# Probability-weighted sums of v with the probabilities as weights, turned back by VectorE, and the last chunk's wide visits at other places

## The chip, the cores and the metric

The kernel runs on one core of one Trainium2 chip. The metric is the time of one execution in device microseconds. TensorE (PE) multiplies, VectorE (DVE) and ScalarE (ACT) do the elementwise work, SyncE (SP) issues nearly all transfers, GpSimd (POOL) makes a few masks.

## The reference, cut to what matters

Attention over 8 batches, 8 heads, 576 positions and a head size of 64, with a window of 32 (heads 0 to 3 plain, heads 4 to 7 with a stride of 4 over 128 positions), and then a feed-forward layer on the result.

```
scores = scale * q @ k^T              # masked: 0 <= rel < 32, or 0 <= rel < 128 and rel % 4 == 0
attn   = exp(scores - max) / (sum + 1e-9)
x      = attn @ v                     # (8, 8, 576, 64), then (4608, 512)
h      = x @ w_in                     # 512 -> 2048
out    = gelu(h) @ w_out              # 2048 -> 512
```

Inputs and results are fp32. q and k are drawn so that the scores spread widely.

## The kernel before

The 4608 rows are worked on in nine chunks (c = 0 to 8) of 512 rows. Chunks 0 to 7 are the first 512 positions of a batch, chunk 8 holds the 64 positions that each batch has left. A chunk's attention is done in four pairs of heads (p = 0, 1 plain, p = 2, 3 strided), each pair in windows of 32 queries by 64 keys; in chunk 8 pairs 2 and 3 are "wide", 32 queries by 96 keys.

The feed-forward layer of a chunk is written out in four quarters of eight steps, 32 in all: eight blocks of `h` (`ffn_h_part`, L530, each block 12 matmuls of 128x512 and then a Gelu on ScalarE and a rounding split on ScalarE and VectorE), eight blocks of `o` (`ffn_o`, L557, 12 such matmuls each), eight more of `h`, and then `o` again, this time one output bank after the other, 24 matmuls each. Every product is done as three matmuls on rounded halves. `h` goes to PSUM banks 4 and 5 in turn, `o` is summed up in banks 0 to 3.

While the layer of chunk c runs, the attention of chunk c + 1 is put between its matmuls, by a list of steps that is sorted by place and then by rank (L667 to L707): `scores` at places 2 and 4 (two pairs at a time), `softmax` on ScalarE from 8.5, the norm and `turn` on VectorE from 10.5, the product with v (`av`, L475) at 24.75 for pairs 0 and 1 and at 26.75 for pairs 2 and 3, and right behind it `xout` (L500), which copies the product as a rounded half (ScalarE) and takes the rest off it (VectorE). These halves are what the next chunk's `h` reads. All queues run in the order in which this list writes them. A visit of two pairs to TensorE is called a burst here. The trace shows each fp32 matmul of the attention as two weight loads and two matmuls, so that a burst of 64 matmuls has 128 of each.

In `scores` a pair's weights are 32 queries of one head (64 rows by 32 columns) and the moving data are 64 keys. In `av` before, the weights are v of one head and window half (64 rows by 64 columns) and the moving data are 32 queries' probabilities; the result stands as head dimension by query, as the layer needs it. In chunk 8 the wide pairs' `av` takes 32 rows by 64 columns as weights, 48 matmuls for half a pair, in four visits, at 26.75 and 28.25 (pair 2) and 28.5 and 30 (pair 3). `av` writes banks 4 to 7; pair p has 128 columns of each.

Chunk 0's attention and the weights' unpacking come first, in an order written out by hand; chunks 0 and 1 use other functions (`av_wide`, `av_early`) for the product with v. The work tiles of a pair (`sm`, `turned`) rotate through seven buffers.

Of the kernel before, what the change touches and what calls it, by code (L numbers as in the profile page):

```python
# [7 lines left out]
F32 = mybir.dt.float32  # L8
# [8 lines left out]
B, H, S, D = 8, 8, 576, 64  # L17
WIN, DIL = 32, 4
DM, DFF = H * D, 2048
P = 128  # L20
# [7 lines left out]
KB, NU = 32, 4  # L28
# [50 lines left out]
def attn_ffn(ctx: ExitStack, tc: tile.TileContext, qk, qk_lp, qk_ld, v, v_ld, w, outT):  # L79
    nc = tc.nc  # L80
# [3 lines left out]
    work = ctx.enter_context(tc.tile_pool(name="work", bufs=2))  # L84
# [3 lines left out]
    ps = psum.tile([P, 8, 512], F32, name="ps")  # L88
# [7 lines left out]
    def copy(e, out, in_):  # L96
        if e == "a":
            nc.scalar.copy(out, in_)  # L98
        else:
            nc.vector.tensor_copy(out, in_)  # L100
# [133 lines left out]
    def load(s):  # L234
        yield "q"
        if s.rest:
            t = wpool.tile([P, N + NU * 4 * KL if s.wide else N + B * KL], F32, tag="w", name="raw_qk")
            src = (qk_ld if s.wide else qk_lp)[s.p % 2]
            s.raw = t
        else:  # L240
            if s.p % 2 == 0:
                held["qk", s.c, s.p // 2] = wpool.tile([P, 2, 2 * N], F32, tag="w", name="raw_qk")
            s.raw = held["qk", s.c, s.p // 2][:, s.p % 2]
            src = qk[s.c, s.p]
        nc.sync.dma_start(s.raw, src)  # L245

    def load_v(s):

        yield "q"
        t = wpool.tile([P, 2, NU, 2, 2 * D], F32, tag="w", name="v_sb")  # L250
        nc.sync.dma_start(t, v[s.c, s.p // 2])
        for i in range(2):
            o = xs[s.c][s.p + i]
            o.v = t[:, i] if s.c > 1 else t[:, i].rearrange("p u j d -> p (u j) d").rearrange("p (a r) d -> p a r d", a=2)
# [13 lines left out]
    def slot(s, u):  # L268
        return u if s.plain or s.rest or s.c < 2 else (u - 1) % NU
# [96 lines left out]
    def sum_up(s):  # L366
        yield "d"
        nc.vector.tensor_reduce(s.st[:, 1], s.all, axis=AX.X, op=ALU.add)
# [71 lines left out]
    def turn_half(s, k):  # L440

        e = yield "ad"
        rows = slice(64 * k, 64 * k + 64)
        copy(e, s.t[rows, :, k], ps[rows, s.bank].rearrange("p (i n) -> p i n", n=KB))
# [27 lines left out]
                            to = to[:, (2 * r + a) * KB:(2 * r + a + 1) * KB]  # L472
                        nc.tensor.matmul(to, s.v[rows, a, r, h * D:(h + 1) * D], t, start=True, stop=True)  # L473

    def av(s, px, u0=0):  # L475

        yield "p"
        s.px = px
        if s.wide:
            for u in range(u0, u0 + 2):  # L480
                for m in range(3):
                    for r in range(4):
                        rows = slice(32 * r, 32 * r + 32)
                        for h in range(2):
                            nc.tensor.matmul(px(r)[h * D:(h + 1) * D, u * KB:(u + 1) * KB], s.v[rows, u, m, h * D:(h + 1) * D],  # L485
                                             s.t[h][rows, 3 * u + m], start=m == 0, stop=m == 2)
            return
        for u in range(NU):
            for j in range(2):
                for r in (j, 2 + j):  # L490
                    rows = slice(r // 2 * 64, r // 2 * 64 + 64)
                    for h in range(2):
                        nc.tensor.matmul(px(r)[h * D:(h + 1) * D, u * KB:(u + 1) * KB], s.v[rows, u, j, h * D:(h + 1) * D],  # L493
                                         s.t[rows, h * NU + slot(s, u), j], start=True, stop=True)

    def px_four(p, bank):

        return (lambda r: ps[:, bank + r, p * P:(p + 1) * P]), ps[:, bank:bank + 4, p * P:(p + 1) * P]

    def xout(s, px):  # L500
        e = yield "ad" if s.c < 2 else "a"
        s.x = xg.tile([P, 2, N], F32R, tag="xg", name="x")
        if s.wide:
            put = []
            for b in range(2):
                src = px[:, :, b * 64:(b + 1) * 64].rearrange("p r (g i) -> p r g i", g=4)
                dst = [s.x[:, t].rearrange("p (r b i g) -> p r b g i", r=4, b=2, g=4)[:, :, b] for t in range(2)]
                put.append((src, dst))
        elif s.c < 2:

            px = ps[:, s.bank + 1] if s.wide_v else ps[:, s.bank:s.bank + 2, s.p % 2 * 256:s.p % 2 * 256 + 256]
            to = [s.x[:, t] if s.wide_v else s.x[:, t].rearrange("p (k n) -> p k n", k=2) for t in range(2)]
            if s.wide_v and s.plain:
                px = px.rearrange("p (b d i) -> p b d i", d=DIL, i=8)
                to = [y.rearrange("p (d b i) -> p b d i", d=DIL, i=8) for y in to]
            put = [(px, to)]
        else:
            put = [(px, [s.x[:, t].rearrange("p (r i) -> p r i" if s.plain or s.rest else "p (i r) -> p r i", r=4)
                         for t in range(2)])]
        for y, (h, l) in put:  # L520
            copy(e, h, y)
        yield "d"
        for y, (h, l) in put:
            nc.vector.tensor_sub(l, y, h)  # L524
# [59 lines left out]
    jobs = {}  # L584
# [3 lines left out]
    def one(e, fns):  # L588

        yield e  # L590
        for g in fns:
            at_once(g)

    for f in range(NF):
# [4 lines left out]
        for i, cols in enumerate(parts(f)):  # L599
            k = f"{f}.{i}" if f < HALVED else f"{f}"  # L600
# [7 lines left out]
    for c in range(3):  # L608
        for p in range(NPAIR):
            s, k = xs[c][p], f"{c}.{p}"  # L610
            jobs["qk" + k] = load(s)
            if c == 2:
                continue
            if p % 2 == 0:
                jobs["v" + k] = load_v(s)
            if c == 0:
                jobs["scores" + k] = scores(s, (4, 0, 2, 6)[p])
                jobs["av" + k] = av_wide(s)
                for i in range(2):
                    jobs[f"half{k}.{i}"] = turn_half(s, i)  # L620
            elif p % 2 == 0:
                jobs["scores" + k] = one("p", [scores(xs[c][p + i], 6) for i in range(2)])
                jobs["av" + k] = one("p", [av_early(xs[c][p + i]) for i in range(2)])
            if c == 0 or p % 2 == 0:
                jobs["low" + k] = lowest_two(s, xs[c][p + 1]) if c else lowest(s)
                jobs["sums" + k] = inverse(s)
            jobs["exp" + k] = softmax(s)
            if s.subtract:
                jobs["sub" + k] = subtract(s)
                jobs["sum" + k] = sum_up(s)  # L630
            jobs["norm" + k] = norm(s)
            jobs["turn" + k] = turn_pe(s)
            jobs["x" + k] = xout(s, None)
    for d in range(NC):
        jobs[f"store0.{d}"] = store(0, d)

# [1 line left out]
    for i in range(BURN):  # L638
        rows = slice(32 * (i % 4), 32 * (i % 4) + 32)
        nc.tensor.matmul(ps[rows, 7, 0:2 * KB], ones[rows, 0:KB], ones[rows], start=True, stop=True)  # L640
    begun, ended, wants = set(), set(), {}
    for token in SCHEDULE.split():
        name, _, times = token.partition("*")
        name, _, e = name.partition(":")
        times = int(times or 1)
        if name == "fill":
            bank = 7
            if "scores0.3" in begun:
                bank = next(k for p, k in ((0, 5), (3, 7), (2, 3), (1, 1)) if f"exp0.{p}" in ended and f"av0.{p}" not in begun)
# [20 lines left out]
    def add(c, at, rank, gen):  # L670
        steps.append((2 * NF * c + at, rank, len(steps), gen))
# [5 lines left out]
                at_once(f)  # L677
        return gen()

    A_SC, A_E, A_N, A_X, A_QK, A_V = (2, 4), 8.5, 10.5, (24.75, 26.75), 26.5, 3  # L680
    for n in range(2, NCH):
        c = n - 1
        s = xs[n]
        late = n == LAST
        for p in range(NPAIR):
            wide = late and p >= 2
            bank = 4 + 2 * (p - 2) if wide else p // 2 * 2
            if c > 1:
                add(c, (3.25 + .25 * (p % 2)) if wide else A_QK - 32 + .25 * p, 0, load(s[p]))
            add(c, A_SC[p // 2] if not wide else 8.25, 1, scores(s[p], bank))  # L690
            add(c, A_SC[p // 2] + .5 + p % 2 if not wide else 8.5 + (p - 2), 2, lowest(s[p]))
            add(c, A_E + p + (.5 if wide else 0), 3, softmax(s[p]))
            add(c, A_N + p * 1.5 + (.5 if wide else 0), 4, inverse(s[p]))
            add(c, A_N + p * 1.5 + (.5 if wide else 0), 4, norm(s[p]))
            add(c, A_N + p * 1.5 + (.5 if wide else 0), 5, turn(s[p]))
            px = px_four(p, 4)
            at = A_X[p // 2] + (1.75 * (p - 2) if wide else 0)
            for u in (range(0, NU, 2) if wide else [0]):
                add(c, at + .75 * u, 6, av(s[p], px[0], u))
            add(c, at + (1.75 if wide else .25 + p % 2 / 2), 7, xout(s[p], px[1]))  # L700
        add(c, A_V, 0, load_v(s[0]))
        if late:
            add(c, 9, 0, load_v_wide(s[2]))
            add(c, 9.25, 0, load_v_wide(s[3]))
        else:
            add(c, A_V + .25, 0, load_v(s[2]))
    steps.sort(key=lambda t: t[:3])  # L707
    at = 0
# [127 lines left out]
```

## Time and profile before

| what | value |
| --- | --- |
| time, median of 3 runs | 886.9 us (885.46 to 887.28) |
| time of the profiled execution | 885.41 us |
| its span in the profile | 883.6 us |
| TensorE busy | 871.6 us, 99% of the span |
| VectorE busy | 352.1 us, 40% |
| ScalarE busy | 380.6 us, 43% |
| granted TensorE clock, mean | 0.999 |

A line of the profile's list of groups names the line of the kernel, the engine, the operation, the tiles (out<-in), partitions by elements, the count, then busy time, mean time of one in ns, and the engine's idle time ahead of them with what ended it. PEld is TensorE's weight load, which runs beside its matmuls. A line of the timeline has the start, the length, the engine, the same names, and in brackets the idle time ahead of it.

### The profile page before, as it was taken

How to read it: one execution, taken by the hardware profiler on the slowest of the kernel's cores; microseconds unless marked ns; L12 is line 12 of the kernel's file. 1: busy time of each engine (PE TensorE's matmuls, PEld its weight loads, DVE VectorE, ACT ScalarE, POOL GpSimd, SP SyncE). 2: the span in 40 equal slices, each digit the busy share in tenths (PEclk: the TensorE clock that was granted, in tenths of full speed). 3: DMA queues.
4: the chain of work that ended last, by engine and by line, in shares of the span. 5: the costliest groups of instructions: out<-in, count | busy, mean ns of one | idle time of the engine just before them, and what ended most of it. 6: DMA issues, size and time to landing. Idle time of an engine off the chain costs nothing.

```text
span 883.6 us, 18852 instructions
## 1 busy us (share of the span) xinstructions
PE 871.6 (99%) x8304; PEld 719.4 (81%) x8304; DVE 352.1 (40%) x597; ACT 380.6 (43%) x1016; POOL 9.5 (1%) x46
## 2 busy tenths in 40 slices
PE   7999999999999999999999999999999999999998
PEld 5888888888888888888888888888888888878886
DVE  8899934621462126321552146213622163212020
ACT  7798535442363227232544235423733272314040
POOL 1000020000000000000000000000000000000000
PEclk9999999999999999999999999999999999999999
DMA  9997431003300330024000510033002410010001
GB/s 363 416 420 281 143 101 46 1 1 134 107 0 1 121 120 1 1 92 148 3 1 1 172 69 0 1 133 108 1 1 85 167 73 1 13 38 1 0 1 48
DMA packets 16930, 75.39 MB, mean 85 GB/s; under 512 B 1872, under 2 KB 2128, under 8 KB 12496
## 3 DMA queue, kind: packets, MB, share of 16 engines
q1 hardware_dynamic: 16704, 74.06, 22.5%
q8 instruction: 65, 1.06, 0.5%
q14 instruction: 17, 0.14, 0.1%
q10 hardware_dynamic: 144, 0.13, 0.0%
HBM read 64.75 MB, written 9.44 MB: 84 GB/s over the span
## 4 chain that ended last, share of the span: by engine, by line
PE 97%; DMA 2%; SPq 0%; issue 0%; DVE 0%; ACT 0%; ACTq 0%; DVEq 0%
PE ps L560 45%; PE ps L537 45%; PE ps L493 3%; PE ps L296 3%; DMA raw_w<-w 2%; PE ps L485 1%; PE ps L473 0%; PE ps L431 0%; PE ps L454 0%; SPq L245 0%; PE ps L282 0%; ACT zeroed L98 0%; SPq L166 0%; DVE spare L190 0%; DVE sm L405 0%
## 5 line engine op out<-in xcount | busy, mean ns | idle before, releaser
L560 PE MATMUL ps<-g,weight 128*128 128x512 f32 x1728 | 401.7, 390 | 0.0
L537 PE MATMUL ps<-x,weight 128*128 128x512 f32 x1728 | 401.3, 390 | 0.0
L537 PEld LDWEIGHTS ps<-x,weight 128*128 128x128 f32 x1728 | 322.9, 188 | 67.9
L560 PEld LDWEIGHTS ps<-g,weight 128*128 128x128 f32 x1728 | 322.9, 188 | 67.2
L549 DVE TENSOR_TENSOR g<-gf,g 128x512 fp32r<-128x512 f32 x144 | 99.7, 693 | 382.6 <-ACT g L98 382.5
L544 ACT ACTIVATE gf<-ps 128x512 f32<-128x512 f32 x144 | 86.1, 598 | 311.1 <-PE ps L537 311.1
L98 ACT CAST g<-gf 128x512 fp32r<-128x512 f32 x143 | 88.8, 621 | 4.5
L380 ACT ACTIVATE sm<-sm,st 128x64 f32<-128x64 f32 (+1 forms) x224 | 74.9, 337 | 0.1
L98 ACT COPY o_sb<-ps 128x512 f32<-128x512 f32 (+1 forms) x34 | 19.7, 582 | 108.4 <-PE ps L560 103.8
L524 DVE TENSOR_TENSOR x<-ps,x 128x512 fp32r<-128x512 f32 (+1 forms) x38 | 30.2, 805 | 86.8 <-ACT x L98 86.8
L98 ACT CAST x<-ps 128x512 fp32r<-128x512 f32 (+1 forms) x37 | 27.0, 749 | 58.9 <-PE ps L493 40.6
L423 DVE STREAM_TRANSPOSE turned<-sm 32x256 f32<-32x256 f32 x104 | 45.4, 436 | 2.0
L380 ACT ACTIVATION_READ_ACCUMULATOR sm<-sm,st 128x1 f32 x224 | 42.1, 188 | 0.0
L296 PEld LDWEIGHTS ps<-raw_qk 64*32 64x32 f32 x2304 | 26.0, 110 | 9.3 <-issue 5.4
L296 PE MATMUL ps<-raw_qk 64*32 64x64 f32 (+1 forms) x2304 | 30.2, 236 | 2.5 <-DMA raw_qk<-qk 2.4
L493 PEld LDWEIGHTS ps<-turned,v_sb 64*64 64x64 f32 x1664 | 25.4, 135 | 4.6 <-issue 4.6
L493 PE MATMUL ps<-turned,v_sb 64*64 64x32 f32 x1664 | 26.9, 220 | 0.0
L405 DVE TENSOR_TENSOR sm<-sm,st 128x512 f32<-128x512 f32 x30 | 20.6, 690 | 0.9
L209 DVE SCALAR_TENSOR_TENSOR weight<-raw_w,spare 128x1024 fp32r<-128x1024 uint32 (+1 forms) x17 | 19.8, 1162 | 0.4
L197 DVE SCALAR_TENSOR_TENSOR raw_w<-raw_w,spare 128x1024 uint32<-128x1024 uint32 (+1 forms) x17 | 19.6, 1155 | 0.0
L418 DVE STREAM_TRANSPOSE turned<-sm 128x512 f32<-128x512 f32 x26 | 18.5, 711 | 0.9
L338 DVE TENSOR_REDUCE st<-sm 128x8 f32<-128x512 f32 x26 | 17.8, 686 | 0.9
(77 smaller groups left out, 252.0 us busy)
## 6 DMA issues: line engine op xcount, KB each, us to landing
v_sb<-v SPq DMA_DIRECT2D x17, 1024.0 KB, 5.2
raw_qk<-qk SPq DMA_DIRECT2D x32, 512.0 KB, 6.8
raw_w<-w SPq DMA_DIRECT2D x15, 1024.0 KB, 17.6
outT<-o_sb SPq DMA_DIRECT2D x35, 256.0 KB, 2.1
mid_w<-w SPq DMA_DIRECT2D x8, 1023.5 KB, 17.6
raw_qk<-qk_ld SPq DMA_DIRECT2D x2, 1024.0 KB, 6.6
v_wide<-v_ld SPq DMA_DIRECT2D x2, 768.0 KB, 6.1
raw_qk<-qk_lp SPq DMA_DIRECT2D x2, 640.0 KB, 5.3
```

Source lines behind the costliest of these rows:

```text
L98: nc.scalar.copy(out, in_)
L209: nc.vector.scalar_tensor_tensor(weight(f)[:, 1, cols], low, 2.0 ** (-36 if f in TWICE or f in MIDDLE else -43), t.bitcast(F32), op0=ALU.m ...
L296: nc.tensor.matmul(s.sc[32 * r:32 * r + 32, h, c0:c0 + s.nk], x[:, q0:q0 + 32], x[:, k0:k0 + s.nk], start=s.c > 1, stop=s.c > 1 or u == NU ...
L380: nc.scalar.activation(t, s.sc[:, i // NU, at:at + 2 * KB] if s.c < 2 else t, AF.Exp, bias=s.st[:, 0, i:i + 1], scale=SCALE if s.c < 2 els ...
L405: nc.vector.tensor_mul(s.all, s.all, t.unsqueeze(2).broadcast_to((P, 2 * NU, 2 * KB)))
L423: nc.vector.transpose(s.t[32 * to:32 * to + 32, :, r % 2], s.all[32 * r:32 * r + 32, :, j * KB:(j + 1) * KB])
L493: nc.tensor.matmul(px(r)[h * D:(h + 1) * D, u * KB:(u + 1) * KB], s.v[rows, u, j, h * D:(h + 1) * D], s.t[rows, h * NU + slot(s, u), j], s ...
L524: nc.vector.tensor_sub(l, y, h)
L537: nc.tensor.matmul(bank, weights[f][:, t, cc * P:(cc + 1) * P], x[:, xx], start=n == 1 and i == 0, stop=n == parts and i == 2)
L544: nc.scalar.activation(gf, bank, AF.Gelu)
L549: nc.vector.tensor_sub(g[:, 1], gf, g[:, 0])
L560: nc.tensor.matmul(ps[:, d], weights[f][:, t, DM + d * P:DM + (d + 1) * P], gs[f][:, u], start=f == 0 and n == 0, stop=f == NF - 1 and n == 2)
```

## The change

In chunks 2 to 7, and in chunk 8 for the plain pairs, `av` exchanges its operands: the probabilities (64 rows by 32 columns) are the weights and v (64 rows by 64 columns) is the moving data. There are as many matmuls as before, 32 for a pair. The result stands as query by head dimension, so a new function `turn_back` transposes it on VectorE in squares of 32 by 32, from PSUM into a new work tile `y` of the seven rotating buffers: six instructions for a pair, two over all 128 partitions and four over 32, each with 256 elements in a partition. `xout` then copies and subtracts from `y` and not from PSUM. A pair's product now takes two banks (4 and 5 for pairs 0 and 2, 6 and 7 for pairs 1 and 3), 256 columns of each. The places of the plain visits stay; `turn_back` has rank 7 and `xout` rank 8, so both pairs' turns stand ahead of both pairs' subtractions. In chunk 8 the four wide visits move to 26.25, 27.5, 29 and 30.25.

```
-                for r in (j, 2 + j):
-                    rows = slice(r // 2 * 64, r // 2 * 64 + 64)
+                for k in range(2):
+                    rows = slice(64 * k, 64 * k + 64)
                     for h in range(2):
-                        nc.tensor.matmul(px(r)[h * D:(h + 1) * D, u * KB:(u + 1) * KB], s.v[rows, u, j, h * D:(h + 1) * D],
-                                         s.t[rows, h * NU + slot(s, u), j], start=True, stop=True)
+                        g = 2 * h + j
+                        nc.tensor.matmul(s.px[32 * g:32 * g + 32, k, u * D:(u + 1) * D], s.t[rows, h * NU + slot(s, u), j],
+                                         s.v[rows, u, j, h * D:(h + 1) * D], start=True, stop=True)
...
+    def turn_back(s):
+        s.y = work.tile([P, 4, NU, KB], F32, tag="sm", name="y", bufs=7)
+        def part(src, dst, d, j):
+            x = s.px[src].rearrange("p r (u d k) -> p r u d k", d=2, k=KB)[:, :, :, d]
+            y = s.y[dst].rearrange("p (r j) u q -> p r u j q", j=2)[:, :, :, j]
+            nc.vector.transpose(y, x)
+        for d in range(2):
+            yield "d"
+            part(slice(0, P), slice(0, P), d, d)
+        for g in range(4):
+            yield "d"
+            part(slice(32 * g, 32 * g + 32), slice(32 * (g ^ 1), 32 * (g ^ 1) + 32), 1 - g % 2, g % 2)
...
-    A_SC, A_E, A_N, A_X, A_QK, A_V = (2, 4), 8.5, 10.5, (24.75, 26.75), 26.5, 3
+    A_SC, A_E, A_N, A_QK, A_V = (2, 4), 8.5, 10.5, 26.5, 3
...
+        A_X = (24.75, 24.75, 26.25, 29) if late else (24.75, 24.75, 26.75, 26.75)
...
-            at = A_X[p // 2] + (1.75 * (p - 2) if wide else 0)
-            for u in (range(0, NU, 2) if wide else [0]):
-                add(c, at + .75 * u, 6, av(s[p], px[0], u))
-            add(c, at + (1.75 if wide else .25 + p % 2 / 2), 7, xout(s[p], px[1]))
+            at = A_X[p]
+            add(c, at, 6, av(s[p]))
+            if wide:
+                add(c, at + 1.25, 6, av(s[p], 2))
+                add(c, at + 1.5, 8, xout(s[p]))
+            else:
+                add(c, at + .25, 7, turn_back(s[p]))
+                add(c, at + .25 + p % 2 / 2, 8, xout(s[p]))
```

TensorE at the second burst of a chunk (pairs 2 and 3 of chunk 2), before, with the engines or transfers that an instruction waits for in brackets:

```order
L560 MATMUL ps<-g,weight 128x512 [waits Activation_49]
L560 MATMUL ps<-g,weight 128x512
L560 MATMUL ps<-g,weight 128x512 [waits DVE_49]
L560 MATMUL ps<-g,weight 128x512 x9
L493 MATMUL ps<-turned,v_sb 64x32 [waits DMAHW6_49,DVE_49]
L493 MATMUL ps<-turned,v_sb 64x32 x63
L560 MATMUL ps<-g,weight 128x512 x63
```

And now:

```order
L578 MATMUL ps<-g,weight 128x512 [waits Activation_49]
L578 MATMUL ps<-g,weight 128x512
L578 MATMUL ps<-g,weight 128x512 [waits DVE_49]
L578 MATMUL ps<-g,weight 128x512 x9
L497 MATMUL ps<-v_sb,turned 32x64 [waits DMAHW6_49,DVE_49]
L497 MATMUL ps<-v_sb,turned 32x64 x31
L497 MATMUL ps<-v_sb,turned 32x64 [waits DVE_49]
L497 MATMUL ps<-v_sb,turned 32x64 x31
L578 MATMUL ps<-g,weight 128x512 x63
```

The burst stands where it stood; its second half, pair 3, has a wait for VectorE of its own.

VectorE at the two bursts of the same chunk, before (L549 are the splits of the last `h` blocks and of the next chunk's first):

```order
L423 STREAM_TRANSPOSE turned<-sm 32x8x32 x3
L549 TENSOR_TENSOR g<-gf,g 128x512 [waits PE_49,Activation_49] x8
L524 TENSOR_TENSOR x<-ps,x 128x512 [waits Activation_49] x2
L524 TENSOR_TENSOR x<-ps,x 128x4x128 [waits Activation_49] x2
L549 TENSOR_TENSOR g<-gf,g 128x512 [waits DVE_49,PE_49,Activation_49] x3
```

And now, from the first burst to behind its subtractions:

```order
L567 TENSOR_TENSOR g<-gf,g 128x512 [waits PE_49,Activation_49] x8
L509 STREAM_TRANSPOSE y<-ps 128x2x128 [waits PE_49]
L509 STREAM_TRANSPOSE y<-ps 128x2x128
L509 STREAM_TRANSPOSE y<-ps 32x2x128 [waits DVE_49] x2
L509 STREAM_TRANSPOSE y<-ps 32x2x128 x2
L509 STREAM_TRANSPOSE y<-ps 128x2x128 [waits PE_49]
L509 STREAM_TRANSPOSE y<-ps 128x2x128
L509 STREAM_TRANSPOSE y<-ps 32x2x128 [waits DVE_49] x2
L509 STREAM_TRANSPOSE y<-ps 32x2x128 x2
L542 TENSOR_TENSOR x<-y,x 128x512 [waits Activation_49] x2
```

Twelve transposes have come in ahead of the two subtractions; the same stands at the second burst.

TensorE in the last quarter ahead of chunk 8, from the first wide visit on, before:

```order
L485 MATMUL ps<-turned,v_wide 64x32 [waits DMAHW2_49,DVE_49]
L485 MATMUL ps<-turned,v_wide 64x32 x47
L560 MATMUL ps<-g,weight 128x512 x18
L485 MATMUL ps<-turned,v_wide 64x32 x48
L560 MATMUL ps<-g,weight 128x512 x3
L485 MATMUL ps<-turned,v_wide 64x32 [waits DMAHW3_49]
L485 MATMUL ps<-turned,v_wide 64x32 x47
L560 MATMUL ps<-g,weight 128x512 x18
L485 MATMUL ps<-turned,v_wide 64x32 [waits DVE_49]
L485 MATMUL ps<-turned,v_wide 64x32 x47
L560 MATMUL ps<-g,weight 128x512 x24
```

And now:

```order
L486 MATMUL ps<-turned,v_wide 64x32 [waits DMAHW2_49,DVE_49]
L486 MATMUL ps<-turned,v_wide 64x32 x3
L486 MATMUL ps<-turned,v_wide 64x32 [waits DVE_49]
L486 MATMUL ps<-turned,v_wide 64x32 x43
L578 MATMUL ps<-g,weight 128x512 x15
L486 MATMUL ps<-turned,v_wide 64x32 x48
L578 MATMUL ps<-g,weight 128x512 x18
L486 MATMUL ps<-turned,v_wide 64x32 [waits DMAHW3_49,DVE_49]
L486 MATMUL ps<-turned,v_wide 64x32 x47
L578 MATMUL ps<-g,weight 128x512 x15
L486 MATMUL ps<-turned,v_wide 64x32 x48
L578 MATMUL ps<-g,weight 128x512 x21
```

The gaps of 18, 3 and 18 matmuls between the wide visits are 15, 18 and 15 now, the first wide visit comes 18 matmuls after the burst of the plain pairs (24 before), and it has a second wait for VectorE.

## Rows read from the trace of the kernel before

**Rows 1.** The page's first part: span, and busy time of each engine.

```profile
span 883.6 us, 18852 instructions
PE 871.6 (99%) x8304; PEld 719.4 (81%) x8304; DVE 352.1 (40%) x597; ACT 380.6 (43%) x1016; POOL 9.5 (1%) x46
```

**Rows 2.** The page's fourth part: the chain that ended last, shares by engine.

```profile
PE 97%; DMA 2%; SPq 0%; issue 0%; DVE 0%; ACT 0%; ACTq 0%; DVEq 0%
```

**Rows 3.** Timeline of TensorE's matmuls: start, length, line, tiles, count; two bursts, one scores visit.

```profile
192.87 2.20 PE L560 MATMUL ps<-g,weight 128*128 128x512 f32 x9
195.00 2.07 PE L493 MATMUL ps<-turned,v_sb 64*64 64x32 f32 x128
197.00 5.74 PE L560 MATMUL ps<-g,weight 128*128 128x512 f32 x24
202.67 2.07 PE L493 MATMUL ps<-turned,v_sb 64*64 64x32 f32 x128
204.67 14.58 PE L560 MATMUL ps<-g,weight 128*128 128x512 f32 x63
219.08 5.60 PE L537 MATMUL ps<-x,weight 128*128 128x512 f32 x24
224.62 1.48 PE L296 MATMUL ps<-raw_qk 64*32 64x64 f32 x128
226.03 5.73 PE L537 MATMUL ps<-x,weight 128*128 128x512 f32 x24
```

**Rows 4.** Groups of instructions: line, engine, operation, tiles, count, busy us, mean ns.

```profile
L493 PEld LDWEIGHTS ps<-turned,v_sb 64*64 64x64 f32 x1664 | 25.4, 135 | 4.6 <-issue 4.6
L493 PE MATMUL ps<-turned,v_sb 64*64 64x32 f32 x1664 | 26.9, 220 | 0.0
```

**Rows 5.** Timeline of TensorE's matmuls ahead of the last chunk.

```profile
763.93 2.07 PE L493 MATMUL ps<-turned,v_sb 64*64 64x32 f32 x128
765.93 5.74 PE L560 MATMUL ps<-g,weight 128*128 128x512 f32 x24
771.59 1.17 PE L485 MATMUL ps<-turned,v_wide 32*64 32x32 f32 x96
772.70 4.38 PE L560 MATMUL ps<-g,weight 128*128 128x512 f32 x18
777.01 1.17 PE L485 MATMUL ps<-turned,v_wide 32*64 32x32 f32 x96
778.11 0.96 PE L560 MATMUL ps<-g,weight 128*128 128x512 f32 x3
779.00 1.00 PE L485 MATMUL ps<-turned,v_wide 32*64 32x32 f32 x76
781.41 0.42 PE L485 MATMUL ps<-turned,v_wide 32*64 32x32 f32 x20 [1.40 <-issue]
781.76 4.37 PE L560 MATMUL ps<-g,weight 128*128 128x512 f32 x18
```

**Rows 6.** The page's third part: the queue that brings instructions.

```profile
q8 instruction: 65, 1.06, 0.5%
```

**Rows 7.** Timeline of ScalarE and VectorE behind the two bursts of Rows 3.

```profile
197.14 0.59 ACT L98 CAST x<-ps 128x512 fp32r<-128x512 f32 x1 [2.82 <-PE ps L493]
...
208.12 1.08 DVE L524 TENSOR_TENSOR x<-ps,x 128x512 fp32r<-128x512 f32 x1 [1.13 <-ACT x L98]
```

**Rows 8.** Timeline of VectorE: the four 32-partition transposes of one pair.

```profile
251.59 1.78 DVE L423 STREAM_TRANSPOSE turned<-sm 32x256 f32<-32x256 f32 x4
```

**Rows 9.** Groups of VectorE's instructions: a transpose, and one operation from PSUM, one from SBUF.

```profile
L423 DVE STREAM_TRANSPOSE turned<-sm 32x256 f32<-32x256 f32 x104 | 45.4, 436 | 2.0
L405 DVE TENSOR_TENSOR sm<-sm,st 128x512 f32<-128x512 f32 x30 | 20.6, 690 | 0.9
L418 DVE STREAM_TRANSPOSE turned<-sm 128x512 f32<-128x512 f32 x26 | 18.5, 711 | 0.9
L332 DVE SCALAR_TENSOR_TENSOR sm<-ps,masks 128x512 f32<-128x512 f32 x24 | 16.4, 684 | 0.0
```

More of the change, by code (lines that the diff above doesn't have):

```diff
@@ L473, in av_early, with av @@
                         nc.tensor.matmul(to, s.v[rows, a, r, h * D:(h + 1) * D], t, start=True, stop=True)
-    def av(s, px, u0=0):
+    def av(s, u0=0):
         yield "p"
-        s.px = px
         if s.wide:
+            s.px = ps[:, 4:8, s.p * P:(s.p + 1) * P]
             for u in range(u0, u0 + 2):
@@ L484, in av, with xout @@
                         for h in range(2):
-                            nc.tensor.matmul(px(r)[h * D:(h + 1) * D, u * KB:(u + 1) * KB], s.v[rows, u, m, h * D:(h + 1) * D],
+                            nc.tensor.matmul(s.px[h * D:(h + 1) * D, r, u * KB:(u + 1) * KB], s.v[rows, u, m, h * D:(h + 1) * D],
                                              s.t[h][rows, 3 * u + m], start=m == 0, stop=m == 2)
             return
+        bank = 4 + s.p % 2 * 2
+        s.px = ps[:, bank:bank + 2, s.p // 2 * NU * D:(s.p // 2 + 1) * NU * D]
         for u in range(NU):
             for j in range(2):
-                for r in (j, 2 + j):
-                    rows = slice(r // 2 * 64, r // 2 * 64 + 64)
+                for k in range(2):
+                    rows = slice(64 * k, 64 * k + 64)
                     for h in range(2):
-                        nc.tensor.matmul(px(r)[h * D:(h + 1) * D, u * KB:(u + 1) * KB], s.v[rows, u, j, h * D:(h + 1) * D],
-                                         s.t[rows, h * NU + slot(s, u), j], start=True, stop=True)
-    def px_four(p, bank):
-        return (lambda r: ps[:, bank + r, p * P:(p + 1) * P]), ps[:, bank:bank + 4, p * P:(p + 1) * P]
-    def xout(s, px):
+                        g = 2 * h + j
[13 more added lines that the diff above has]
+            part(slice(32 * g, 32 * g + 32), slice(32 * (g ^ 1), 32 * (g ^ 1) + 32), 1 - g % 2, g % 2)
+    def xout(s):
         e = yield "ad" if s.c < 2 else "a"
@@ L505, in xout @@
             for b in range(2):
-                src = px[:, :, b * 64:(b + 1) * 64].rearrange("p r (g i) -> p r g i", g=4)
+                src = s.px[:, :, b * 64:(b + 1) * 64].rearrange("p r (g i) -> p r g i", g=4)
                 dst = [s.x[:, t].rearrange("p (r b i g) -> p r b g i", r=4, b=2, g=4)[:, :, b] for t in range(2)]
@@ L517, in xout @@
         else:
-            put = [(px, [s.x[:, t].rearrange("p (r i) -> p r i" if s.plain or s.rest else "p (i r) -> p r i", r=4)
-                         for t in range(2)])]
+            put = [(s.y.rearrange("p r u q -> p r (u q)"),
+                    [s.x[:, t].rearrange("p (r i) -> p r i" if s.plain or s.rest else "p (i r) -> p r i", r=4) for t in range(2)])]
         for y, (h, l) in put:
@@ L632, in attn_ffn @@
             jobs["turn" + k] = turn_pe(s)
-            jobs["x" + k] = xout(s, None)
+            jobs["x" + k] = xout(s)
     for d in range(NC):
@@ L695, in attn_ffn @@
             add(c, A_N + p * 1.5 + (.5 if wide else 0), 5, turn(s[p]))
-            px = px_four(p, 4)
-            at = A_X[p // 2] + (1.75 * (p - 2) if wide else 0)
-            for u in (range(0, NU, 2) if wide else [0]):
-                add(c, at + .75 * u, 6, av(s[p], px[0], u))
-            add(c, at + (1.75 if wide else .25 + p % 2 / 2), 7, xout(s[p], px[1]))
+            at = A_X[p]
[6 more added lines that the diff above has]
+                add(c, at + .25 + p % 2 / 2, 8, xout(s[p]))
         add(c, A_V, 0, load_v(s[0]))
```

## The prediction

> **What bounds the kernel now.** I read the busy times first: TensorE is busy for 871.6 of 883.6 us, VectorE for 40% and ScalarE for 43% [rows 1]. The chain of work that ended last then says the same of the end: 97% of it is TensorE, and no other engine has one per cent of it [rows 2]. So an edit counts by what it takes from TensorE's queue or makes that queue wait, and work on VectorE is free as long as TensorE doesn't wait for it. Third, TensorE's timeline around one chunk, which gives each kind of visit its price, start to start of what follows: the burst of two pairs of `av` takes 195.00 to 197.00, 2.00 us, and the visit of two pairs of `scores` 224.62 to 226.03, 1.41 us, for as many weight loads and matmuls, 128 each [rows 3]. Fourth, the same timeline ahead of chunk 8, which holds a place where TensorE stood still [rows 5].
>
> **The new burst.** The list of groups has 1664 matmuls in `av` at L493, 128 to a burst, so 13 bursts: two in each of chunks 2 to 7 and one in chunk 8 [rows 4]. The change keeps their count and exchanges the operands. The new shape, weights of 64 by 32 and 64 columns of data, is just the shape of `scores` [rows 3], down to one PSUM bank for each half of the rows. What differs is the order: `scores` changes the half of the rows at each matmul, the new loop at every second. The wide visits of chunk 8 also do two matmuls in a row on the same rows, and take 771.59 to 772.70, 1.11 us, for 96 [rows 5], which is 1.48 us for 128. So the burst lies between 1.41 and 1.48 us; I take 1.41, since `scores` has the very tile. Gain: 13 x (2.00 - 1.41) = 7.7 us (6.8 us with 1.48). All of it lies on the path.
>
> **The wide visits.** The first two took 1.11 and 1.10 us. The third began at 779.00, stopped after 76 of 96, waited 1.40 us for nothing that the profile shows, and let the next work begin at 781.76: 2.76 us, 1.65 us too long [rows 5]. It is the visit that came only 3 large matmuls behind another. The queue that brings instructions moved 65 packets [rows 6], and TensorE's 8304 matmuls and 8304 loads [rows 1] are 65 times 256: I read the stop as TensorE running out of instructions, with some 350 of them used up in the 3.0 us from 777.01 to 780.0. Now 15, 18 and 15 large matmuls lie between the visits. A gap of 18 had no stop [rows 5]; one of 15 isn't in the trace and lies nearer to 18 than to 3. I take the whole stop as gone: 1.65 us gained, with nought as the other end.
>
> **VectorE's new work.** Six transposes a pair, 26 pairs. Four transposes of 256 elements take 1.78 us back to back [rows 8], 0.445 us each; one over 128 partitions of 512 elements takes 711 ns against 436 [rows 9], so 256 elements cost the same on 32 or on 128 partitions within what these rows show. That is 26 x 6 x 0.445 = 69 us on an engine that is 60% idle. The rows are all from SBUF, and the new ones read PSUM; the nearest pair of rows is an operation of 512 elements from PSUM, 684 ns, beside one from SBUF, 690 ns [rows 9], so I add nothing. [...]
>
> **The waits it adds.** The instruction order shows two for TensorE. Say a first burst starts at S. Pair 0's half ends 0.7 us later, plus 0.22 us for the last matmul [rows 4] and 0.07 us to the reader (ScalarE began at 197.14 after an end at 197.07 [rows 3, 7]): VectorE begins at S + 1.0 and, with twelve transposes, is done at S + 6.3. The second burst starts behind 24 large matmuls, 197.00 to 202.67, 5.67 us [rows 3], so at S + 7.1, and its second half, which is what waits for the twelfth transpose, at S + 7.8. Slack: 1.4 us, and no wait. Queued behind that wait would be all of TensorE's work; it starts to cost at (7.8 - 1.1) / 12 = 0.56 us a transpose. Ahead of chunk 8 it is closer: the first wide visit comes 18 large matmuls behind the burst, 772.70 to 777.01, 4.31 us [rows 5], so at S + 5.7, and its fifth matmul writes a bank that pair 1's transposes read until S + 6.3, seen by TensorE at about S + 6.4. Cost: 0.7 us, once (nothing if a transpose takes under 0.39 us).
>
> Further on nothing is late. Today's subtractions end at 208.12 + 1.08 = 209.2 and the next `h`, which needs them, starts at 219.08 [rows 3, 7]; twelve transposes, two copies and two subtractions behind the second burst take about 7.5 us from its end, with 14.4 us to that `h`. The copies hold back one store of an output bank behind them on ScalarE by 2 us, and that bank is next written at 224.62. The seven rotating buffers get 12 tiles a chunk in place of 8; the buffer that `y` takes was last read by transposes or a burst ahead of it. No transfer moves past another on SP, and POOL has nothing to do with it.
>
> **Sum.** -7.7 - 1.65 + 0.7 = -8.6 us. The profiled execution took 885.41 us with a span of 883.6; its span should come to 875.0 and its time to 876.8. It lay 1.5 us below the median of the runs, 886.9, so for the median I say **878.3 us**.
>
> **Rivals.**
> *VectorE becomes the wait (slower).* Place: the second half of the second burst in chunks 2 to 7, and the first wide visit. With t us a transpose each of the six second bursts waits 12t - 6.7, the wide visit 12t - 4.7. The gain ahead of waits is 9.3 us, so it turns to a loss from t = 0.64 on. If reading PSUM in squares paid the 275 ns twice that 256 elements cost between the two rows for transposes [rows 9], t = 0.72, the waits are 6 x 1.9 + 3.9 = 15.5 us, the sum is +6, and the time 893. For it: no row has a transpose from PSUM. Against: the operations that do read it cost no more.
> *The burst doesn't get faster.* If its pace hangs on the order of the rows and not on the tile, which `av` before and after share, only the stop goes: -1.65 + 0.3 for the wide wait, 885.6. Against: the wide visits have that order too, at 11.6 ns a matmul in place of 15.6.
> *The burst halves.* Eight tiles for four would make it 1.00 us: 13.0 + 1.65 - 0.8, 873. Against: `scores` has the eight tiles already and takes 1.41 [rows 3]. [...]
> *The stop stays.* A gap of 15 may still be too short, or the shorter bursts ahead may shift where it falls: -7.7 + 0.7, 879.9.
>
> **How the numbers follow.** Forecast, with its own bounds for burst and wait, 0.80; the stop stays 0.07; VectorE late 0.06, of which 0.04 beyond the point where it is a loss; no faster burst 0.05; the burst halves 0.02. A measurement of this kernel can tell about 0.2%, 1.8 us, from no change. So faster: 0.80 + 0.07 + 0.02 + 0.02 = 0.91; same: the unchanged burst, 0.05; slower: 0.04. The forecast's own range is 877.5 (no wide wait) to 879.9 (burst at 1.48, PSUM dearer); the median of three runs lay within 1.5 us of each. So 876.0 to 881.0, which takes in the stop that stays.
>
> **What would show it.** In the new profile: bursts of L497 that take 1.41 to 1.48 us; VectorE's twelve transposes done 6.3 us after a burst's start, at about 0.445 us each, and no wait of TensorE for them at the second bursts; one wait of some 0.7 us in the first wide visit; four wide visits of 1.1 us and no idle time without a releaser; VectorE busy for about 420 us. Wrong is the prediction if the burst stays near 2 us, if L497 waits for VectorE in each chunk, or if a stop turns up in a burst that had none.

## The result and the profile after

The changed kernel takes 877.5 us, median of 4 runs (877.16 to 878.18), beside 886.18 us for the kernel before (885.39 to 887.28): a ratio of 0.9902, 95% interval 0.9885 to 0.9919. The forecast was 878.3 us, within 876.0 to 881.0. The profiled execution took 877.81 us with a span of 876.0 (forecast: 876.8 and 875.0). Of ten executions of the kernel before that were timed beside the first experiments, six had a mean granted clock of 0.998 and took 887.0 to 887.1 us, four 0.999 or 1.000 and took 885.0 to 885.8: that is the 1.5 us by which its profile lay below its median.

The page's first part of the changed kernel, to be laid beside [rows 1]:

```profile
span 876.0 us, 19002 instructions
PE 865.6 (99%) x8304; PEld 711.6 (81%) x8304; DVE 419.2 (48%) x753; ACT 379.7 (43%) x1016; POOL 9.5 (1%) x46
```

TensorE is still busy for 99% of the span, with as many instructions, and VectorE has 156 more instructions and 67 us more work. The chain that ended last has a new share, against [rows 2]:

```profile
PE 97%; DMA 2%; DVE 1%; SPq 0%; ACT 0%; issue 0%; ACTq 0%; DVEq 0%
```

VectorE's 1% in it is one place, the first wide visit, shown below. TensorE's timeline at the stretch of [rows 3]:

```profile
195.51 1.48 PE L497 MATMUL ps<-v_sb,turned 64*32 64x64 f32 x128
196.92 5.78 PE L578 MATMUL ps<-g,weight 128*128 128x512 f32 x24
202.63 1.48 PE L497 MATMUL ps<-v_sb,turned 64*32 64x64 f32 x128
204.04 14.62 PE L578 MATMUL ps<-g,weight 128*128 128x512 f32 x63
```

The burst goes from 195.51 to 196.92: 1.41 us, where it was 2.00. VectorE behind it, to be laid beside [rows 7]:

```profile
196.41 5.30 DVE L509 STREAM_TRANSPOSE y<-ps 128x256 f32<-128x256 f32 x12 [0.85 <-PE ps L497]
...
201.74 1.35 DVE L542 TENSOR_TENSOR x<-y,x 128x512 fp32r<-128x512 f32 x2
...
208.86 2.24 DVE L542 TENSOR_TENSOR x<-y,x 128x512 fp32r<-128x512 f32 x2
```

VectorE starts 0.90 us after the burst does, while its second half still runs, and has done all twelve transposes at 201.71, 0.9 us ahead of the second burst and 1.6 us ahead of that burst's half which waits for the twelfth. The last subtraction ends at 211.1; the next `h` starts at 218.50. And ahead of chunk 8, at the stretch of [rows 5]:

```profile
758.12 1.48 PE L497 MATMUL ps<-v_sb,turned 64*32 64x64 f32 x128
759.53 4.42 PE L578 MATMUL ps<-g,weight 128*128 128x512 f32 x18
763.88 0.32 PE L486 MATMUL ps<-turned,v_wide 32*64 32x32 f32 x8
764.37 1.11 PE L486 MATMUL ps<-turned,v_wide 32*64 32x32 f32 x88 [0.18 <-DVE y L509]
765.41 3.69 PE L578 MATMUL ps<-g,weight 128*128 128x512 f32 x15
769.03 1.18 PE L486 MATMUL ps<-turned,v_wide 32*64 32x32 f32 x96
770.13 4.37 PE L578 MATMUL ps<-g,weight 128*128 128x512 f32 x18
```

The stop of 1.40 us is gone. In its place the first wide visit breaks off after 8 of 96 matmuls until pair 1's transposes are done; it takes 763.88 to 765.41, 1.53 us, 0.42 us more than the 1.11 us of the others.

### The profile page after: what moved, and what is told of

Its sections match the earlier page's. It is cut to its first block, busy times and chain, and to the rows that moved or that the text cites. A ratio compares the mean times of both kernels' runs of the same rounds, so it can differ in the third digit from the quotient of the medians.

```text
span 876.0 us, 19002 instructions
## 1 busy us (share of the span) xinstructions
PE 865.6 (99%) x8304; PEld 711.6 (81%) x8304; DVE 419.2 (48%) x753; ACT 379.7 (43%) x1016; POOL 9.5 (1%) x46
## 4 chain that ended last, share of the span: by engine, by line
PE 97%; DMA 2%; DVE 1%; SPq 0%; ACT 0%; issue 0%; ACTq 0%; DVEq 0%
PE ps L555 45%; PE ps L578 45%; PE ps L296 3%; PE ps L497 2%; DMA raw_w<-w 2%; DVE y L509 1%; PE ps L486 1%; PE ps L473 0%; PE ps L431 0%; PE ps L454 0%; SPq L245 0%; PE ps L282 0%; ACT zeroed L98 0%; SPq L166 0%; DVE spare L190 0%
## 5 line engine op out<-in xcount | busy, mean ns | idle before, releaser
L509 DVE STREAM_TRANSPOSE y<-ps 128x256 f32<-128x256 f32 (+1 forms) x156 | 66.7, 440 | 10.8 <-PE ps L497 8.6
L98 ACT CAST x<-y 128x512 fp32r<-128x512 f32 x26 | 22.0, 847 | 73.5 <-DVE y L509 73.5
L542 DVE TENSOR_TENSOR x<-y,x 128x512 fp32r<-128x512 f32 x26 | 22.6, 879 | 0.7
L497 PEld LDWEIGHTS ps<-v_sb,turned 64*32 64x32 f32 x1664 | 17.2, 105 | 4.6 <-issue 2.5
L497 PE MATMUL ps<-v_sb,turned 64*32 64x64 f32 x1664 | 19.3, 225 | 0.0
```

Source lines behind the costliest of these rows:

```text
L497: nc.tensor.matmul(s.px[32 * g:32 * g + 32, k, u * D:(u + 1) * D], s.t[rows, h * NU + slot(s, u), j], s.v[rows, u, j, h * D:(h + 1) * D], ...
L509: nc.vector.transpose(y, x)
```

## Experiments

**The two parts apart.** First the exchange alone, with the wide visits at their old places:

```
-        A_X = (24.75, 24.75, 26.25, 29) if late else (24.75, 24.75, 26.75, 26.75)
+        A_X = (24.75, 24.75, 26.75, 28.5) if late else (24.75, 24.75, 26.75, 26.75)
...
-                add(c, at + 1.25, 6, av(s[p], 2))
-                add(c, at + 1.5, 8, xout(s[p]))
+                add(c, at + 1.5, 6, av(s[p], 2))
+                add(c, at + 1.75, 8, xout(s[p]))
```

> The exchanged operands with VectorE's turning back, and the wide visits at the places of the kernel before (gaps of 18, 3 and 18 large matmuls, 24 ahead of the first). My theory: 13 bursts of 1.41 us in place of 2.00 give 7.7 us; with 24 matmuls ahead of the first wide visit the twelfth transpose is early enough (done 6.2 us after the burst's start, needed at 7.2) and there is no wait; the stop of TensorE in the third wide visit is back, some 1.4 us of idle time that nothing explains. Some 1.2 us slower than the changed kernel: about 878.7 us, 0.9915 of before. Rival, that the stop hung on where the slower bursts left the supply of instructions: no stop, 877.1 us.

Measured: 878.53 us, ratio 0.9911 (0.9898 to 0.9925). TensorE's timeline ahead of chunk 8:

```profile
769.79 1.17 PE L486 MATMUL ps<-turned,v_wide 32*64 32x32 f32 x96
770.90 0.96 PE L578 MATMUL ps<-g,weight 128*128 128x512 f32 x3
771.79 0.97 PE L486 MATMUL ps<-turned,v_wide 32*64 32x32 f32 x73
773.96 0.43 PE L486 MATMUL ps<-turned,v_wide 32*64 32x32 f32 x23 [1.19 <-issue]
774.32 4.38 PE L578 MATMUL ps<-g,weight 128*128 128x512 f32 x18
```

The stop is back at the third visit, after 73 of 96 matmuls in place of 76, and the visit takes 2.53 us. The wait for VectorE is gone, as 24 large matmuls stand ahead of the first wide visit again. Then the wide visits' new places alone, in the kernel before:

```
-            at = A_X[p // 2] + (1.75 * (p - 2) if wide else 0)
+            at = (26.25, 29)[p - 2] if wide else A_X[p // 2]
...
-                add(c, at + .75 * u, 6, av(s[p], px[0], u))
-            add(c, at + (1.75 if wide else .25 + p % 2 / 2), 7, xout(s[p], px[1]))
+                add(c, at + .625 * u, 6, av(s[p], px[0], u))
+            add(c, at + (1.5 if wide else .25 + p % 2 / 2), 7, xout(s[p], px[1]))
```

> The kernel before with only the four wide visits moved to their new places (gaps of 15, 18 and 15). My theory: the stop goes and nothing else changes, 1.65 us less than before, 0.998 of it: about 884.5 us. Each chunk between the third and the last still takes 94.8 us from burst to burst, each burst 2.00 us. Rival, that the stop moves to another visit: 886.2 us and an idle time without a releaser somewhere.

Measured: 883.9 us, ratio 0.9975 (0.9963 to 0.9986). All four visits take 1.10 to 1.11 us, with no idle time that lacks a releaser, and the first `h` of chunk 8 comes 27.19 us after the plain pairs' burst (764.27 to 791.46), where it was 28.81 (763.93 [rows 5] to 792.74): 1.62 us, forecast 1.65. So the exchange carries about 0.9% and the spread 0.25%. That is 1.14% together, where both at once gave 0.98%: the wait in the first wide visit, 0.42 us, is 0.05% of the difference, and the rest lies within the intervals.

**Tile or order of the rows.** The order of the loop in the new product, so that each matmul changes the half of the rows:

```
-                for k in range(2):
-                    rows = slice(64 * k, 64 * k + 64)
-                    for h in range(2):
-                        g = 2 * h + j
+                for h in range(2):
+                    g = 2 * h + j
+                    for k in range(2):
+                        rows = slice(64 * k, 64 * k + 64)
```

> The changed kernel with the loop over the halves of the rows innermost in the product with v, so that each matmul changes the half as in the scores. My theory, that the tile sets the pace: a burst takes 1.41 us as before this edit, 877.5 us. Rival, that the order of the rows counts: another burst, down to 1.2 us, and 13 x 0.2 = 2.6 us less.

Measured, in one execution: 876.82 us, and the burst takes 1.41 us as it did (195.19 to 196.60):

```profile
195.19 1.48 PE L497 MATMUL ps<-v_sb,turned 64*32 64x64 f32 x128
196.60 5.74 PE L578 MATMUL ps<-g,weight 128*128 128x512 f32 x24
```

The same in the kernel before, whose weights are 64 by 64:

```
-                for r in (j, 2 + j):
-                    rows = slice(r // 2 * 64, r // 2 * 64 + 64)
-                    for h in range(2):
+                for h in range(2):
+                    for r in (j, 2 + j):
+                        rows = slice(r // 2 * 64, r // 2 * 64 + 64)
```

> The kernel before with the same reordering of its product with v: the half of the rows changes at each matmul, weights still 64 by 64. My theory, that the tile (four of them, 64 columns of weights each) sets the pace of the burst: 2.00 us still, and 886.2 us. Rival, that its order of rows made it slow: near 1.41 us, 7.7 us less, 878.5 us.

Measured: 886.05 us, ratio 0.9999 (0.9990 to 1.0009); the burst goes from 195.24 to 197.23, 1.99 us:

```profile
195.24 2.07 PE L493 MATMUL ps<-turned,v_sb 64*64 64x32 f32 x128
197.23 5.74 PE L560 MATMUL ps<-g,weight 128*128 128x512 f32 x24
```

Neither product cares for the order. The new product also writes two banks for a pair, where the old one wrote four. The early chunks' product (`av_early`, L473) tells these apart in the trace of the kernel before: its tile is the old one, weights of 64 by 64 and 32 columns of data, but it writes two banks for a pair, and it takes 94.98 to 96.98, 2.00 us:

```profile
94.98 2.07 PE L473 MATMUL ps<-turned,v_sb 64*64 64x32 f32 x128
96.98 3.02 PE L537 MATMUL ps<-x,weight 128*128 128x512 f32 x12
```

So what is left to make 2.00 into 1.41 is the operands' shapes, weights of 64 by 32 and 64 columns of data against 64 by 64 and 32. The 64 columns of weights alone are not it: the wide visits have them too, with 32 columns of data and only 32 rows, and take 11.6 ns a matmul where the old product takes 15.6 [rows 3, 5]. Why the one shape is faster than the other stays open.

**What the stop was.** The first burst of chunks 2 to 7 done twice in a row, the second time over the same result:

```
             add(c, at, 6, av(s[p]))
+            if p < 2 and not late:
+                add(c, at, 6.5, av(s[p]))
```

> The changed kernel with the first burst of chunks 2 to 7 done twice in a row (the second time writes the same values again), 512 small TensorE instructions in a row in place of 256. What it tells: whether the stop of the kernel before was TensorE running out of instructions. If so, each of the six doubled bursts has idle time without a releaser inside, some 1 to 2 us, and the kernel takes 6 x (1.41 + 1.5) = 17 us more, 895 us. Rival, that the stop belonged to the place ahead of the last chunk: 6 x 1.41 = 8.5 us more, 886 us, with no idle time in the burst.

Measured, in one execution: 904.07 us. The waits of TensorE show one entry of idle time without a releaser, six times, once in each doubled burst, and the timeline has the first two of them:

```profile
PE ps L497 <- issue: 11.6, 6, 2.4
```

```profile
195.23 2.11 PE L497 MATMUL ps<-v_sb,turned 64*32 64x64 f32 x192
199.16 0.86 PE L497 MATMUL ps<-v_sb,turned 64*32 64x64 f32 x64 [1.82 <-issue]
...
292.14 2.09 PE L497 MATMUL ps<-v_sb,turned 64*32 64x64 f32 x190
296.35 0.88 PE L497 MATMUL ps<-v_sb,turned 64*32 64x64 f32 x66 [2.11 <-issue]
297.16 7.30 PE L578 MATMUL ps<-g,weight 128*128 128x512 f32 x24
```

From the third part of its page, the queue that brings instructions:

```profile
q8 instruction: 71, 1.16, 0.5%
```

That is 6 packets more than [rows 6], for 6 x 128 more weight loads and as many more matmuls: 256 instructions a packet, as the prediction read it. In the 8 us around the first stop (192 to 200) one packet of this queue is all that the transfers' view has:

```profile
DMA packets 1, 0.02 MB, mean 2 GB/s; under 512 B 0, under 2 KB 0, under 8 KB 0
...
q8 instruction: 1, 0.02, 0.7%
```

The stop therefore does not belong to the place ahead of the last chunk, nor to a transfer of data. In the doubled bursts it comes after 368 to 384 small instructions in a row; in the kernel before it came after 344, with three large matmuls among them. This stop ends 2.4 us after one packet of the instruction queue has moved (at 196.8, and TensorE goes on at 199.16), and the one in the kernel before 2.2 us after (a packet at 779.2, and on at 781.41). It is TensorE running out of instructions as far as these views can tell; that it waits for just this packet is inferred, since the packet has moved before the stop begins (197.34 here, 780.00 in the kernel before).

**VectorE's room.** Each transpose out of PSUM done twice:

```
-            nc.vector.transpose(y, x)
+            for _ in range(2):
+                nc.vector.transpose(y, x)
```

> The changed kernel with each of VectorE's transposes out of PSUM done twice, 12 a pair in place of 6, with the same result. My theory: the change is for nothing only as long as VectorE is done in time. Its 24 transposes end 0.9 + 24 x 0.445 = 11.6 us after the first burst's start; the second half of the second burst would start at 7.8, so TensorE waits 3.8 us in each of six chunks, and 5.7 us in place of 0.4 in the first wide visit: 28 us more, about 905 us. Rival, that VectorE's share of 48% leaves room for it: 877.5 us and no wait of TensorE.

Measured, in one execution: 921.03 us. TensorE's waits and its timeline at the stretch of [rows 3], with the same stretch by windows (busy time of each engine, granted clock, share of the transfers, GB/s):

```profile
PE ps L497 <- DVE y L510: 24.3, 6, 4.1
PE ps L486 <- DVE y L510: 5.9, 2, 5.2
```

```profile
202.28 0.86 PE L497 MATMUL ps<-v_sb,turned 64*32 64x64 f32 x64
207.18 1.11 PE L497 MATMUL ps<-v_sb,turned 64*32 64x64 f32 x64 [4.05 <-DVE y L510]
208.22 15.70 PE L579 MATMUL ps<-g,weight 128*128 128x512 f32 x63
```

```profile
202.00:207.00 5.00, 1.13 (x66) 0.70 (x64) 4.74 (x12) 0.24 (x1) 0.00 (x0) 1.00 0.02 3
207.00:210.00 3.00, 2.82 (x68) 2.36 (x69) 2.87 (x7) 1.10 (x2) 0.00 (x0) 0.55 0.30 100
210.00:214.00 4.00, 4.00 (x17) 3.25 (x16) 3.81 (x9) 0.00 (x0) 0.00 (x0) 0.91 0.92 284
```

The waits are near the forecast ones, 4.05 us six times for 3.8, and 5.9 us for 5.7. But the whole is 43.2 us more than the changed kernel's profiled execution, and the waits make 30 of them. The rest is TensorE's clock: behind the wait the granted clock is 0.55 for 3 us and 0.91 for the 4 us after them, and the work there takes longer. The 63 large matmuls took 15.5 us, 14.5 in the changed kernel, and the half burst 1.04 in place of 0.70. In the other five chunks the 63 took 15.3 to 16.8 us; over all six, with the first wide visit and the 15 large matmuls behind it, such lengthening adds up to some 13 us, which is the rest. To tell the wait from the clock, nine transposes a pair in place of six:

```
-        for d in range(2):
+        for d in (0, 1, 0, 1, 1):
```

> The changed kernel with nine transposes out of PSUM a pair in place of six (the two over all partitions are repeated, one of them twice; same result). It separates the wait of TensorE from what came on top of it with twelve, where each wait of 4.05 us was followed by a stretch at a low clock. My theory: 18 transposes end 0.9 + 18 x 0.455 = 9.1 us after the first burst's start, TensorE's second half of the second burst could start at 7.8, so it waits 1.3 us in each of six chunks and 3.3 us in place of 0.4 in the first wide visit, and its clock holds after the short waits: 877.3 + 7.8 + 2.9 = 888 us, with at most one drop of the clock, behind the long wait (1.7 us more). Rival, that any wait there costs clock as well: 6 x 1.7 us more, 898 us.

Measured, in one execution: 885.78 us.

```profile
PE ps L497 <- DVE y L509: 3.6, 6, 0.6
PE ps L486 <- DVE y L509: 2.5, 1, 2.5
```

```profile
195.99 7.59 DVE L509 STREAM_TRANSPOSE y<-ps 128x256 f32<-128x256 f32 x18 [0.85 <-PE ps L497]
```

```profile
770.55 1.11 PE L486 MATMUL ps<-turned,v_wide 32*64 32x32 f32 x88 [2.49 <-DVE y L509]
771.59 5.30 PE L578 MATMUL ps<-g,weight 128*128 128x512 f32 x15
```

I had put 0.455 us on a repeated transpose; 18 took 7.59 us, 0.42 each. With that the sum works: 0.9 + 7.59 = 8.5 us after the burst's start against 7.8, and the wait is 0.6 to 0.7. The clock held behind those six, where the 63 large matmuls took 14.4 us, and fell once, behind the 2.49 us: it is 0.80 from 772 to 780, and 15 large matmuls took 5.2 us there, 3.6 elsewhere. The rival, a fall behind any wait, is out for waits of 0.59 us; the forecast waits of 1.3 us did not come about, so nothing here shows what one of that length costs.

**A version without the wide wait.** The changed kernel with the first two wide visits a quarter of a step later:

```
-        A_X = (24.75, 24.75, 26.25, 29) if late else (24.75, 24.75, 26.75, 26.75)
+        A_X = (24.75, 24.75, 26.5, 29) if late else (24.75, 24.75, 26.75, 26.75)
```

> The changed kernel with the first two wide visits a quarter of a step later (21 large matmuls ahead of the first in place of 18, gaps of 15, 15 and 15). My theory: TensorE reaches the fifth matmul of the first wide visit some 6.5 us after the burst's start, behind the twelfth transpose (6.2 us), so the wait of 0.4 us there is gone: 877.1 us, too little to be told from the changed kernel by the times, but visible in the trace. Rival: the gap of 15 between the second and third visit brings the stop back, 878.5 us.

Measured: 877.21 us, ratio 0.9893 (0.9878 to 0.9908). The wait is gone (first visit 765.25 to 766.35) and the stop does not come back with gaps of 15, 15 and 15:

```profile
765.25 1.17 PE L486 MATMUL ps<-turned,v_wide 32*64 32x32 f32 x96
766.35 3.70 PE L578 MATMUL ps<-g,weight 128*128 128x512 f32 x15
```

From the plain pairs' burst to the first `h` of chunk 8 it takes 26.62 us (758.83 to 785.45) where the changed kernel takes 27.04 (758.12 to 785.16): the 0.42 us. It is the best of these versions by that, though the times cannot tell it from the changed kernel.

## Why the prediction was right, point by point

- **The bound.** That only TensorE's queue counts held: VectorE got 67 us more work (forecast 69) and the end moved by TensorE's own savings.
- **The burst.** Forecast 1.41 us from the visit of `scores`, measured 1.41, 13 times. That the same tile means the same pace, whatever the order of the rows, was a choice between 1.41 and 1.48; the two reorderings settle it. The rival of a halved burst is out by 0.41 us a burst: eight tiles for four gave a factor of 1.42, not two.
- **The stop.** Forecast 1.65 us, measured 1.62 by the spread alone. Its cause was argued in the prediction from packets and counts; the doubled burst bears it out, as far as the views go.
- **VectorE's price.** 0.445 us a transpose from SBUF rows; from PSUM twelve took 5.30 us, 0.442 each. By shape of the changed kernel's groups:

```profile
L509 DVE STREAM_TRANSPOSE y<-ps 32x256 f32<-32x256 f32 x104 | 46.4, 446 | 1.9
L509 DVE STREAM_TRANSPOSE y<-ps 128x256 f32<-128x256 f32 x52 | 20.3, 428 | 9.0 <-PE ps L497 8.6
```

  446 ns over 32 partitions stand against 436 from SBUF [rows 9]: 10 ns dearer. The dearer PSUM that raises the upper end of the forecast's range to 879.9 is a term that no run shows: in its place twelve transposes out of PSUM took 0.04 us less than twelve at the 0.445 us from SBUF, by their share of 128-partition ones at 428 ns.
- **The waits.** None at the second bursts: VectorE was done 1.6 us ahead, forecast 1.4. In the first wide visit 0.42 us, forecast 0.7: VectorE began 0.1 us earlier than I had it and took 0.04 us less, and TensorE reached the visit 0.06 us later.
- **The sum.** The median's closeness is in part luck. The profiled span came out 1.0 us above the forecast, 876.0 for 875.0. For the median I had added the 1.5 us by which the profile of the kernel before lay below its median; the changed kernel's profiled execution lay 0.3 us above its own, so the median came out 0.8 us below the forecast. Profile against profile the gain was 7.6 us of span, forecast 8.6. By stretches, against the kernel before: up to the first burst +0.51 us (195.51 and 195.00 [rows 3]), which nothing in the change touches; from there to the burst ahead of chunk 8 -6.32 us where six chunks of two bursts should give -7.1; from there to the `h` of chunk 8 -1.77 us, forecast -1.5; behind it nothing. The 0.8 us missing in the middle are large matmuls that took a little longer between the bursts in this execution (24 of them 5.71 us, 5.67 before). In the exchange alone the same stretch is 6.88 us shorter than before, in the reordered one 7.04, so most of the 0.8 us is this execution's; why its large matmuls were slower is open.
- **The rivals.** VectorE as the wait was priced at 12t - 6.7 us for each second burst. With twelve transposes a pair the wait came as worked out; what I left out is the clock, which made it dearer. The point from which it loses, put at 0.64 us a transpose, can only be nearer for that; no run shows by how much, as the clock held behind waits of 0.59 us and fell behind the 2.49 us of the wide visit.

## What to carry to other kernels

Choose which operand of a small matmul is the weight by the shapes that another stage already shows in the trace: the same tile cost the same here to a hundredth of a microsecond, 1.41 us a burst. Work that goes to an idle engine was free here only up to the moment at which the bound engine next asked for it (5.30 us of transposes cost no wait at the second burst, 11.04 us of them 4.05 us): compute that moment from the trace, in microseconds after the hand-over, and not from busy shares. And spread long runs of small instructions on TensorE among large ones, since it stood still in them here, 1.2 to 2.4 us at a time, with nothing in the list of waits but idle time without a releaser.

## What the runs showed of the hardware that was not expected

A pause of TensorE can cost more than itself. Where each wait was 4.05 us the granted clock fell in all six chunks: it is 0.97 or 0.98 in each stretch of 100 us that holds one of the waits and 1.00 in the 100 us ahead, 0.55 in the 3 us behind the first, and the 63 large matmuls behind took 15.3 to 16.8 us in place of 14.5. Behind 0.59 us it never fell (14.4 us), nor behind the single stops of 1.40 us in the kernel before (1.00 from 781.4 to 784) and 1.19 us in the exchange alone (18 large matmuls took 4.30 us behind it, 4.31 ahead of it). Behind the stops of the doubled burst it fell in four of six chunks: 24 large matmuls took 7.2 to 7.3 us there (with a clock of 0.79 from 298 to 304) and 5.7 in the other two, and the stops behind which it fell, 2.11, 1.69, 2.43 and 1.86 us, are not all longer than the ones behind which it held, 1.82 and 1.72. What decides between the two is open. So those 17 us that I expected of the doubled bursts became 26: the stops were 11.6 us for the 9 expected, and the lowered clock cost some 6 us.

A doubled burst stopped after 192, 190, 189, 187, 186 and 184 of its 256 matmuls, a little earlier in each chunk, as it would if instructions came in blocks of fixed length and a chunk were a few instructions longer than a whole number of them. That fits the count, though no view shows a block's ends: with the doubled burst a chunk has 1024 weight loads and as many matmuls, eight times 256 instructions, and its other instructions come on top. It would also mean that the six stops are not six independent trials: each doubled burst would have met the blocks at nearly the same point.
